# Retention and bilinear FFN on one core: q and k loads that exchange heads, GpSimd on 128 partitions, large buffers at multiples of 512 bytes

## The chip, the cores and the metric

One core of one Trainium2 chip. The metric is the device time of the kernel in microseconds. The engines are TensorE (PE, its weight loads PEld), VectorE (DVE), ScalarE (ACT), GpSimd (POOL) and SyncE (SP), which only issues DMAs here.

## The reference

```
B, H, S, D = 8, 8, 576, 64
scores = q @ k^T / sqrt(D)
gamma  = 1 - 2 ** (-5 - arange(H))
ret    = scores * where(i >= j, gamma ** (i - j), 0)      # i: query, j: key
x      = (ret @ v) with heads side by side -> [B*S, 512]   # 4608 tokens
out    = ((x @ w_a) * (x @ w_b)) @ w_out                   # 512 -> 1536 -> 512
```

Inputs and output are float32, and the kernel multiplies in bf16.

## The kernel before

The retention is computed in its recurrent form: inside a stretch of 64 tokens by scores, across stretches by a state of 64 x 64 per head. Tokens go in pairs of 128-token tiles (256 tokens). Pairs 0 to 5 belong to the first three batches; 15 and 17 (`LEFT`) collect the last 64 tokens of four batches each. The FFN runs in blocks of 512 tokens. It is PE's main work; three later blocks form sums of weights and rows on DVE, so that PE needs fewer products (`layer_mixed`, `rows_mixed`).

The program's order on every engine is written out by hand. `todo` is a list of places, counted in matmuls of 512 columns, at which `ahead`, `turn`, `stretch`, `load_pair` and `store_held` are called while the FFN's matmuls are issued. For a pair `n`:

- `load_pair(n)` issues the loads of q, k and v on SP (L171). `rows_of` gives two tiles of 128 tokens, or four of 64 for 15 and 17. A tile of `[128, 1024]` float32 holds two such tiles, each with its 8 heads of 64. The staging pool has two buffers per tensor.
- `ahead(n)` prepares operands on POOL: from pair 6 (`MIXED`) on it multiplies q by the decay table `qs2` (`decayed_queries`, L579 and L584), casts k (L605 and L609), and multiplies v by `vs2` (L616). Tokens of the second 64 partitions have the two heads of each couple exchanged in `qkb` (index `1 - r` written from `r`). So POOL works on partitions 0 to 63 and 64 to 127 in separate instructions.
- `turn(n)` transposes `qkb` by two DMAs on SP (L633) into `qkT`, and from pair 11 on then calls `load_pair(n + 2)`.
- `stretch(n, n - 1)` issues PE's products of the pair: `keyed` (L664), `matched` (scores, L735), `open_outputs` (L763) and `close_outputs` (L776).

SP takes its DMAs strictly in order, so pair 13's loads stand before pair 12's transposes. The DMAs of SP use eight semaphores in turn: each one first waits until the eighth before it has landed.

The opening (steps `STEPS`, loads L182) handles the first pairs with dummy matmuls (`warm`) between, until about 18 us. Weights come by POOL's own queue (`load_w`, `load_wo`). `pair_tables` makes `qs2` and `vs2` on ACT from `idxv`, one step at a time in the first FFN block.

`const` is the first pool in each partition's memory, and all large pools follow it. The tiles of `const` add up so that the first large buffer starts at byte 21824 of a partition, 320 past a multiple of 512; the large buffers all keep that offset.

Of the kernel before, what the change touches and what calls it, by code (L numbers as in the profile page):

```python
# [10 lines left out]
FP32 = mybir.dt.float32  # L11
BF16 = mybir.dt.bfloat16
INT32 = mybir.dt.int32
AF = mybir.ActivationFunctionType
# [4 lines left out]
def kernel(  # L19
# [10 lines left out]
    nc = tc.nc  # L30

    B, H, S, D = q.shape
    DM = H * D
# [4 lines left out]
    HP = H // 2  # L38
    scale = 1.0 / math.sqrt(D)
    gammas = [1.0 - 2.0 ** (-5.0 - h) for h in range(H)]  # L40
# [5 lines left out]
    LEFT = {NP - 3: 0, NP - 1: 1}  # L46
# [5 lines left out]
    PAIRS = [(0, 0), (1, 0), (2, 0), (0, 1), (1, 1), (2, 1)]  # L52
# [6 lines left out]
    def part_of(n):  # L59
        return PAIRS[n][1]  # L60
# [4 lines left out]
    def rows_of(n):  # L65

        if n not in LEFT:
            b, m = PAIRS[n]
            return [(kp, 0, 128, b, 256 * m + 128 * kp) for kp in (0, 1)]
        return [(i // 2, 64 * (i % 2), 64, 4 * LEFT[n] + i, S - 64)  # L70
                for i in range(4)]

    def pool(name, bufs, space=None):
        kw = {} if space is None else {"space": space}
        return ctx.enter_context(tc.tile_pool(name=name, bufs=bufs, **kw))

    const = pool("const", 1)
# [67 lines left out]
    def half(i):  # L145
        return slice(64 * i, 64 * i + 64)
# [10 lines left out]
    def staged(n, name, its_name):  # L157

        extra = n < MIXED + 3 and n % 3 == 2
        return (begin if extra else stage).tile(  # L160
            [128, 2 * DM], FP32, tag=name, name=its_name)

    def load_pair(n, which=(0, 1, 2)):
        if n >= NP:
            return
        paired.setdefault(n, {})
        for i in which:
            name, src = (("qf", q), ("kf", k), ("vf", v))[i]
            t = staged(n, name, name + "2")
            for kp, r0, m, b, s0 in rows_of(n):  # L170
                nc.sync.dma_start(  # L171
                    t[r0:r0 + m, kp * DM:(kp + 1) * DM]
                    .rearrange("p (h d) -> p h d", h=H),
                    src[b, :, s0:s0 + m, :].rearrange("h s d -> s h d"))
            paired[n][i] = t

    def load_step(n, hh, which, on=nc.sync):
# [11 lines left out]
    Q, K, V = 0, 1, 2  # L189
# [36 lines left out]
    idxp_f = const.tile([128, 2], FP32)  # L226
    nc.vector.tensor_copy(idxp_f, idxp_i)
    lgp = const.tile([128, HP], FP32)
    for c in range(HP):
        nc.vector.memset(lgp[0:64, c:c + 1], math.log(gammas[2 * c]))  # L230
        nc.vector.memset(lgp[64:128, c:c + 1], math.log(gammas[2 * c + 1]))
    biasq = const.tile([128, 1], FP32)
    nc.vector.memset(biasq, math.log(scale))
    vs = const.tile([128, H, 2], FP32)
    for h in range(H):
        nc.scalar.activation(vs[:, h, :], idxp_f, AF.Exp,
                             bias=0.0, scale=-math.log(gammas[h]))
# [10 lines left out]
    idxv = const.tile([128, 3, 2], FP32)  # L248
    vs2 = const.tile([128, 3, 2, H], FP32)

    qs2 = const.tile([128, 3, 2, H], FP32)
# [14 lines left out]

    def pair_tables(step):
        if step == 0:
            nc.vector.tensor_copy(idxv, idxv_i)
            nc.vector.tensor_scalar_add(idxv[:, 2, 1:2], idxv[:, 2, 1:2],  # L270
                                        -128.0)
            nc.vector.tensor_scalar_add(idxv[64:128, 2], idxv[64:128, 2],
                                        -64.0)
        else:
            for h in (2 * step - 2, 2 * step - 1):
                nc.scalar.activation(vs2[:, :, :, h], idxv, AF.Exp,
                                     bias=0.0, scale=-math.log(gammas[h]))
                nc.scalar.activation(qs2[:, :, :, h], idxv, AF.Exp,
                                     bias=biasq[:, 0:1],
                                     scale=math.log(gammas[h]))  # L280

    state_after = begin.tile([128, 2, HP, 128], BF16)
    own_sums = [begin.tile([128, HP, 64], FP32, name=f"own{n}")
# [280 lines left out]
    def ahead(n):  # L564


        qkb = nat.tile([128, 2, 2 * DM], BF16, tag="qkb", name="qkb2")
        vb = nat.tile([128, 2 * DM], BF16, tag="vb", name="vb2")
        halves = [slice(0, DM), slice(DM, 2 * DM)]
        whole = [slice(0, 2 * DM)]  # L570
        part = 2 if n in LEFT else part_of(n)

        def per_head(t):
            return t.rearrange("p (h d) -> p h d", d=D)

        def decayed_queries(t):
            by = qs2[:, part].rearrange("p k h -> p (k h)")
            for hs in (slice(0, H), slice(H, 2 * H)):
                nc.gpsimd.tensor_tensor(  # L579
                    per_head(qkb[0:64, Q])[:, hs], per_head(t[0:64])[:, hs],  # L580
                    by[0:64, hs].unsqueeze(2).to_broadcast([64, H, D]),
                    op=ALU.mult)
            for r in (0, 1):
                nc.gpsimd.tensor_tensor(  # L584
                    per_head(qkb[64:128, Q])[:, 1 - r::2],
                    per_head(t[64:128])[:, r::2],
                    by[64:128, r::2].unsqueeze(2).to_broadcast([64, H, D]),
                    op=ALU.mult)

        if n >= MIXED:  # L590
            decayed_queries(paired[n].pop(Q))
        if n >= BY_ACT:
            t = paired[n].pop(K)
            to, fro = (x.rearrange("p (j r d) -> p j r d", r=2, d=D)
                       for x in (qkb[64:128, K], t[64:128]))
            key_casts[n] = [
                lambda: nc.scalar.copy(qkb[0:64, K], t[0:64])] + [
                lambda r=r: nc.scalar.copy(to[:, :, 1 - r], fro[:, :, r])
                for r in (0, 1)]
            copies_due.extend([lambda: key_casts[n].pop(0)() if key_casts[n]  # L600
                               else None] * 3)
        for w in () if n >= BY_ACT else (K,) if n >= MIXED else (Q, K):
            t = paired[n].pop(w)
            for e in halves:
                nc.gpsimd.tensor_copy(qkb[0:64, w, e], t[0:64, e])  # L605
                to, fro = (x.rearrange("p (j r d) -> p j r d", r=2, d=D)
                           for x in (qkb[64:128, w, e], t[64:128, e]))
                for r in (0, 1):
                    nc.gpsimd.tensor_copy(to[:, :, 1 - r], fro[:, :, r])  # L609
        t = paired[n].pop(V)  # L610
        decay = (vs2[:, part].unsqueeze(3)
                 .to_broadcast([128, 2, H, D])
                 .rearrange("p k h d -> p (k h) d"))
        for e in halves:
            at = slice(e.start // D, e.stop // D)
            nc.gpsimd.tensor_tensor(  # L616
                vb[:, e].rearrange("p (h d) -> p h d", d=D),
                t[:, e].rearrange("p (h d) -> p h d", d=D),
                decay[:, at], op=ALU.mult)
        natural[FIRST + n, "pair"] = (qkb, vb)  # L620
# [4 lines left out]
    def turn(n):  # L625
        while key_casts.get(n):
            key_casts[n].pop(0)()
        qkb = of(natural, n)[0]
        qkT = qkt_pool.tile([128, 2, 2, HP, 128], BF16, tag="qkT",
                            name="qkT2")  # L630
        transposed[FIRST + n, "pair"] = qkT
        for w in (Q, K):
            nc.sync.dma_start_transpose(  # L633
                qkT[:, w].rearrange("p k c s -> p (k c) s"), qkb[:, w])
        if n > 10:
            load_pair(n + 2)
# [824 lines left out]


    gate = const.tile([1, 64], BF16)
    fence = const.tile([128, 2], FP32)

    def warm(count, n):

# [82 lines left out]
    for i, which in ((4, Q), (4, K), (4, V), (5, Q), (5, K), (5, V)):  # L1550
        load_step(*STEPS[i], which)
    load_pair(FIRST)
    load_pair(FIRST + 1, (Q,))


# [56 lines left out]
    todo += [(150 + 15 * step, weight_sums, (step,)) for step in range(15)]  # L1612
    todo += [(136, total_of, (2,))]
    todo += [(28 + 6 * step, pair_tables, (step,)) for step in range(5)]
    todo += [(145 + 6 * step, decays_next, (step,)) for step in range(5)]
    todo += [(170, stretch, (3, None)), (201, stretch, (4, 3)),
# [33 lines left out]
    for fn, places in ((ahead, casts), (turn, turns)):  # L1650
        todo += [(at, fn, (n,)) for n, at in places.items()]
# [46 lines left out]
```

## Time and profile before

| | us |
|---|---|
| median of 3 runs | 314.54 (314.4 to 314.97) |
| the profiled execution | 314.71 |
| its span | 313.0 |
| PE busy | 303.0 |
| DVE busy | 224.0 |
| POOL busy | 202.8 |
| ACT busy | 156.0 |
| granted clock of PE, share | 0.998 |

The span is what the profile covers of the execution, from the first to the last instruction. The page divides it in 40 slices, where each digit is the busy share in tenths. The tables by line give busy time, the mean of one instruction in ns, and the idle time of the engine just before it with what ended it. Matmuls overlap their neighbours, so one matmul's own time is longer than the distance to the next.

Where the pairs lie in this trace: POOL prepares pair 12 from 153.82 us and pair 17 from 230.83 us. PE's scores (L735) of pairs 11 to 17 begin at 162.50, 174.16, 194.29, 206.07, 226.18, 237.65 and 259.48 us.

### The profile page before, as it was taken

How to read it: one execution, taken by the hardware profiler on the slowest of the kernel's cores; microseconds unless marked ns; L12 is line 12 of the kernel's file. 1: busy time of each engine (PE TensorE's matmuls, PEld its weight loads, DVE VectorE, ACT ScalarE, POOL GpSimd, SP SyncE). 2: the span in 40 equal slices, each digit the busy share in tenths (PEclk: the TensorE clock that was granted, in tenths of full speed). 3: DMA queues.
4: the chain of work that ended last, by engine and by line, in shares of the span. 5: the costliest groups of instructions: out<-in, count | busy, mean ns of one | idle time of the engine just before them, and what ended most of it. 6: DMA issues, size and time to landing. Idle time of an engine off the chain costs nothing.

```text
span 313.0 us, 9645 instructions
## 1 busy us (share of the span) xinstructions
PE 303.0 (97%) x3922; PEld 198.6 (63%) x3955; DVE 224.0 (72%) x450; ACT 156.0 (50%) x351; POOL 202.8 (65%) x290
## 2 busy tenths in 40 slices
PE   7899999999999999999999999999999999999994
PEld 3554457868544554557874787468746875687774
DVE  5745337758757765768878886888679968877873
ACT  7755346626433554455455545544635554335530
POOL 3990079665996649867799769985999350035413
PEclk9999999999999999999999999999999999999999
DMA  8999999999999999999999989948703020013004
GB/s 213 256 202 207 247 240 198 197 216 182 208 171 231 174 204 191 218 244 285 190 260 228 179 180 227 192 83 182 213 10 70 24 112 2 2 53 85 1 2 134
DMA packets 144797, 50.97 MB, mean 163 GB/s; under 512 B 126576, under 2 KB 141680, under 8 KB 144752
## 3 DMA queue, kind: packets, MB, share of 16 engines
q1 hardware_dynamic: 138272, 45.10, 70.9%
q0 software_dynamic: 5808, 4.72, 9.6%
q8 instruction: 31, 0.51, 0.7%
q10 hardware_dynamic: 672, 0.52, 0.5%
q14 instruction: 14, 0.11, 0.1%
HBM read 37.75 MB, written 9.44 MB: 151 GB/s over the span
## 4 chain that ended last, share of the span: by engine, by line
PE 91%; DVE 2%; DMA 2%; SPq 2%; issue 2%; ACT 1%; DVEq 0%; ACTq 0%
PE m L1047 16%; PE pb L1419 13%; PE pa L1398 12%; PE pb L1284 9%; PE pa L1284 9%; PE po L1445 8%; PE lm L1227 7%; PE ls L1227 3%; DMA qf<-in_q_dram 2%; SPq L182 2%; PE la L1227 2%; PE po L933 2%; PE sc L735 2%; PE o L763 1%; PE kv L664 1%
## 5 line engine op out<-in xcount | busy, mean ns | idle before, releaser
L1424 DVE TENSOR_TENSOR hT<-ha,pb 128x512 bf16<-128x512 bf16 (+1 forms) x60 | 34.6, 579 | 32.4 <-PE pb L1419 28.4
L1419 PE MATMUL pb<-xT,wb_sb 128*128 128x512 bf16 (+1 forms) x237 | 49.9, 336 | 0.3
L1398 PE MATMUL pa<-xT,wa_sb 128*128 128x512 bf16 (+1 forms) x238 | 47.6, 326 | 0.5 <-issue 0.3
L1412 ACT CAST ha<-pa 128x512 bf16<-128x512 f32 (+1 forms) x60 | 29.8, 500 | 34.3 <-PE pa L1398 31.8
L1071 POOL TENSOR_TENSOR osb<-crossed,straight 128x256 f32<-128x256 f32 x24 | 17.5, 756 | 44.3 <-ACT crossed L1059 44.3
L1419 PEld LDWEIGHTS <-wb_sb 128*128 128x128 bf16 x240 | 23.4, 98 | 17.8 <-issue 0.5
L1398 PEld LDWEIGHTS <-wa_sb 128*128 128x128 bf16 x244 | 23.3, 98 | 16.5 <-DVE sums L691 0.2
L579 POOL TENSOR_TENSOR qkb<-qf,qs 64x512 bf16<-64x512 f32 x24 | 24.7, 1044 | 13.1 <-DMA qf<-in_q_dram 8.2
L1284 PE MATMUL pb<-xT,wb_sb 128*128 128x512 bf16 x125 | 32.1, 379 | 0.2
L616 POOL TENSOR_TENSOR vb<-vf,vs 128x512 bf16<-128x512 f32 x30 | 30.8, 1046 | 2.0 <-DMA vf<-in_v_dram 0.8
L1284 PE MATMUL pa<-xT,wa_sb 128*128 128x512 bf16 x119 | 31.4, 379 | 0.7 <-issue 0.3
L1047 PEld LDWEIGHTS <-hT 128*128 128x128 bf16 x288 | 28.1, 98 | 5.0 <-DVE hT L981 0.5
L1294 ACT CAST ha<-pa 128x512 bf16<-128x512 f32 x32 | 18.7, 585 | 24.6 <-PE pa L1284 24.6
L1297 DVE TENSOR_TENSOR hT<-ha,pb 128x512 bf16<-128x512 bf16 x32 | 21.9, 684 | 10.0 <-PE pb L1284 8.1
L609 POOL CAST qkb<-kf 64x256 bf16<-64x256 f32 x60 | 27.7, 488 | 1.5
L1445 PE MATMUL po<-wo_sb,hT 128*128 128x512 bf16 x113 | 26.7, 379 | 0.8 <-issue 0.6
L584 POOL TENSOR_TENSOR qkb<-qf,qs 64x512 bf16<-64x512 f32 x24 | 26.7, 1134 | 0.7
L1047 PE MATMUL m<-wo_sums,hsum 128*128 128x256 bf16 x216 | 25.7, 273 | 0.0
L981 DVE TENSOR_TENSOR hsum<-hT 128x512 bf16<-128x512 bf16 (+2 forms) x51 | 23.5, 493 | 0.5
L605 POOL CAST qkb<-kf 64x512 bf16<-64x512 f32 x30 | 20.3, 677 | 5.4 <-DMA kf<-in_k_dram 4.0
L1047 PEld LDWEIGHTS <-hsum 128*128 128x128 bf16 x216 | 21.1, 98 | 2.4
L1284 PEld LDWEIGHTS <-wb_sb 128*128 128x128 bf16 x128 | 12.3, 98 | 14.3
(159 smaller groups left out, 578.4 us busy)
## 6 DMA issues: line engine op xcount, KB each, us to landing
qf<-in_q_dram SPq DMA_DIRECT2D x32, 256.0 KB, 5.4
vf<-in_v_dram SPq DMA_DIRECT2D x32, 256.0 KB, 5.0
kf<-in_k_dram SPq DMA_DIRECT2D x31, 256.0 KB, 5.1
out_dram<-osb SPq DMA_DIRECT2D x9, 512.0 KB, 4.2
out_dram<-osb SPq DMA_DIRECT2D x22, 128.0 KB, 2.8
wo_sb<-in_moe_w_out_dram POOLq DMA_DIRECT2D x3, 512.0 KB, 15.9
out_dram<-osb SPq DMA_DIRECT2D x6, 256.0 KB, 4.1
qf<-in_q_dram SPq DMA_DIRECT2D x8, 128.0 KB, 3.3
```

The lines of the kernel that those rows point to most:

```text
L579: nc.gpsimd.tensor_tensor(per_head(qkb[0:64, Q])[:, hs], per_head(t[0:64])[:, hs], by[0:64, hs].unsqueeze(2).to_broadcast([64, H, D]), op= ...
L584: nc.gpsimd.tensor_tensor(per_head(qkb[64:128, Q])[:, 1 - r::2], per_head(t[64:128])[:, r::2], by[64:128, r::2].unsqueeze(2).to_broadcast( ...
L609: nc.gpsimd.tensor_copy(to[:, :, 1 - r], fro[:, :, r])
L616: nc.gpsimd.tensor_tensor(vb[:, e].rearrange("p (h d) -> p h d", d=D), t[:, e].rearrange("p (h d) -> p h d", d=D), decay[:, at], op=ALU.mult)
L1047: nc.tensor.matmul(to, rows, cols, start=(begins and p == 0), stop=True, skip_group_check=True)
L1227: nc.tensor.matmul(to[:, m], w[:, c], x[:, c], start=(way in (1, 2, 5) and m == c == 0), stop=True, skip_group_check=True)
L1284: nc.tensor.matmul(p1, w[:, c, F * 128:F * 128 + 128], xT[:, c], start=(c == 0), stop=(c == NC - 1))
L1398: nc.tensor.matmul(pa[:, at:at + width], wa_sb[:, c, fs], xT[:, c, at:at + width], start=(c == at == 0), stop=(c == NC - 1), skip_group_ch ...
L1412: nc.scalar.copy(ha[:, 0:n], pa[:, 0:n])
L1419: nc.tensor.matmul(pb[:, 0:n], wb_sb[:, c, fs], xT[:, c], start=(c == 0), stop=(c == NC - 1))
L1424: nc.vector.tensor_tensor(hT[:, F, 0:n], has[F][:, 0:n], pb[:, 0:n], op=ALU.mult)
L1445: nc.tensor.matmul(po, hT[:, F, u * 128:(u + 1) * 128], wo_sb[:, F], start=(F == 0), stop=(F == NF - 1))
```

## The change

From pair 12 (`PLACED`) on, the loads of q and k bring the heads to their exchanged places: `places_of` splits each tile of 128 tokens in three DMAs, one for the first 64 partitions with all heads, and two for the other 64 with four heads each. POOL then multiplies q and casts k on all 128 partitions at once. As the table is now read at the place where a head lies after the exchange, `qs2` gets its rates per partition, from `lgp` for even heads and from a new `lgq`, made by eight memsets on DVE, for odd ones; the older loop for pairs 6 to 11 reads the table at `1 - r`. The tile `fence` becomes part of a tile `room` of 48 columns. With `lgq` (a step of 32 bytes) and `room` the large buffers start at byte 22016, a multiple of 512.

```
+    PLACED = 12
+    def places_of(n, t, src):
+        heads = t.rearrange("p (k j r d) -> p k j r d", k=2, r=2, d=D)
+        if n in LEFT:
+            b0 = 4 * LEFT[n]
+            lower, upper = (src[b0 + a:b0 + 4:2, :, S - 64:S, :].rearrange(
+                "k (j r) s d -> s k j r d", r=2) for a in (0, 1))
+        else:
+            b, m = PAIRS[n]
+            lower, upper = (src[b, :, 256 * m:256 * m + 256, :].rearrange(
+                "(j r) (k a s) d -> a s k j r d", a=2, k=2, r=2)[a]
+                for a in (0, 1))
+        k = (0, 1)
+        return [(to[:, ks], fro[:, ks]) for ks in k for to, fro in (
+            (heads[0:64].rearrange("p k j r d -> p k (j r) d"),
+             lower.rearrange("s k j r d -> s k (j r) d")),
+            (heads[64:128, :, :, 1], upper[:, :, :, 0]),
+            (heads[64:128, :, :, 0], upper[:, :, :, 1]))]
...
     def load_pair(n, which=(0, 1, 2)):
...
+            if i == V or n < PLACED:
+                for kp, r0, m, b, s0 in rows_of(n):
...
+            else:
+                for to, fro in places_of(n, t, src):
+                    nc.sync.dma_start(to, fro)
...
+    lgq = const.tile([128, HP], FP32)
...
     def pair_tables(step):
         if step == 0:
+            for c in range(HP):
+                for i in (0, 1):
+                    nc.vector.memset(lgq[half(i), c:c + 1],
+                                     math.log(gammas[2 * c + 1 - i]))
...
-                nc.scalar.activation(qs2[:, :, :, h], idxv, AF.Exp,
-                                     bias=biasq[:, 0:1],
-                                     scale=math.log(gammas[h]))
+                nc.scalar.activation(
+                    qs2[:, :, :, h], idxv, AF.Exp, bias=biasq[:, 0:1],
+                    scale=(lgq if h % 2 else lgp)[:, h // 2:h // 2 + 1])
...
         def decayed_queries(t):
             by = qs2[:, part].rearrange("p k h -> p (k h)")
+            own = slice(0, 128 if n >= PLACED else 64)
             for hs in (slice(0, H), slice(H, 2 * H)):
                 nc.gpsimd.tensor_tensor(
-                    per_head(qkb[0:64, Q])[:, hs], per_head(t[0:64])[:, hs],
-                    by[0:64, hs].unsqueeze(2).to_broadcast([64, H, D]),
+                    per_head(qkb[own, Q])[:, hs], per_head(t[own])[:, hs],
+                    by[own, hs].unsqueeze(2).to_broadcast([own.stop, H, D]),
                     op=ALU.mult)
-            for r in (0, 1):
+            for r in () if n >= PLACED else (0, 1):
                 nc.gpsimd.tensor_tensor(
                     per_head(qkb[64:128, Q])[:, 1 - r::2],
                     per_head(t[64:128])[:, r::2],
-                    by[64:128, r::2].unsqueeze(2).to_broadcast([64, H, D]),
+                    by[64:128, 1 - r::2].unsqueeze(2).to_broadcast([64, H, D]),
                     op=ALU.mult)
...
             for e in halves:
+                if n >= PLACED:
+                    nc.gpsimd.tensor_copy(qkb[:, w, e], t[:, e])
+                    continue
...
-    fence = const.tile([128, 2], FP32)
+    room = const.tile([128, 48], FP32)
+    fence = room[:, 0:2]
```

More of the change, by code (lines that the diff above doesn't have):

```diff
@@ L169, in load_pair @@
             t = staged(n, name, name + "2")
[L170 to L174, printed above, removed]
+            if i == V or n < PLACED:
+                for kp, r0, m, b, s0 in rows_of(n):
+                    nc.sync.dma_start(
+                        t[r0:r0 + m, kp * DM:(kp + 1) * DM]
+                        .rearrange("p (h d) -> p h d", h=H),
+                        src[b, :, s0:s0 + m, :].rearrange("h s d -> s h d"))
+            else:
+                for to, fro in places_of(n, t, src):
+                    nc.sync.dma_start(to, fro)
             paired[n][i] = t
```

## The prediction

> **What bounds the kernel now.** First the page, for the engines' shares and the slices:
>
> ```profile
> span 313.0 us, 9645 instructions
> PE 303.0 (97%) x3922; PEld 198.6 (63%) x3955; DVE 224.0 (72%) x450; ACT 156.0 (50%) x351; POOL 202.8 (65%) x290
> ...
> PE   7899999999999999999999999999999999999994
> ...
> POOL 3990079665996649867799769985999350035413
> ...
> DMA  8999999999999999999999989948703020013004
> ```
>
> PE fills the span: 303.04 of 313.00 us. GpSimd (POOL) and the DMA engines are also full in long stretches. So I asked for the busy time of the engines by stretch (columns: length, then PE, PEld, DVE, ACT, POOL):
>
> ```profile
> 18.00:40.00 22.00, 21.89 (x103) 10.10 (x104) 8.56 (x15) 9.97 (x29) 6.11 (x13) 1.00 1.25 223
> 40.00:150.00 110.00, 108.42 (x1621) 66.67 (x1635) 76.48 (x147) 55.48 (x124) 82.17 (x120) 1.00 1.13 211
> 150.00:250.00 100.00, 99.31 (x1361) 70.57 (x1369) 81.22 (x150) 51.93 (x106) 83.50 (x106) 1.00 0.75 155
> 250.00:309.00 59.00, 58.55 (x582) 42.75 (x584) 44.73 (x109) 26.00 (x54) 18.30 (x26) 1.00 0.13 43
> ```
>
> The six pairs that the change touches are prepared between 142 and 241 us. There PE lacks 0.69 us in 100. Next, what PE waited for between 18 and 300 us, in whole:
>
> ```profile
> PE po L1445 <- issue: 0.6, 4, 0.2
> PE pa L1398 <- issue: 0.3, 2, 0.2
> PE pa L1284 <- issue: 0.3, 2, 0.2
> ```
>
> No wait of PE there ends with POOL, with SP or with a DMA. A faster POOL has nothing to shorten on PE. What remains outside PE is 1.5 us at the start, about 1.7 us until 18 us, 2.8 us in crumbs after that, and 3.9 us from PE's last matmul (309.1) to the end.
>
> **POOL's part.** The costs come from the page:
>
> ```profile
> L579 POOL TENSOR_TENSOR qkb<-qf,qs 64x512 bf16<-64x512 f32 x24 | 24.7, 1044 | 13.1 <-DMA qf<-in_q_dram 8.2
> L616 POOL TENSOR_TENSOR vb<-vf,vs 128x512 bf16<-128x512 f32 x30 | 30.8, 1046 | 2.0 <-DMA vf<-in_v_dram 0.8
> L609 POOL CAST qkb<-kf 64x256 bf16<-64x256 f32 x60 | 27.7, 488 | 1.5
> L584 POOL TENSOR_TENSOR qkb<-qf,qs 64x512 bf16<-64x512 f32 x24 | 26.7, 1134 | 0.7
> L605 POOL CAST qkb<-kf 64x512 bf16<-64x512 f32 x30 | 20.3, 677 | 5.4 <-DMA kf<-in_k_dram 4.0
> ```
>
> 64 partitions cost what 128 do: L579 (64x512) 1044 ns, L616 (128x512) 1046. For q, 2 x 1.044 + 2 x 1.134 = 4.36 us become 2 x 1.05 = 2.1. For k, 2 x 0.677 + 4 x 0.488 = 3.31 become 2 x 0.61 (the 128x512 cast of L371) = 1.2. That is 4.3 us a pair and 26 us for six. Its worth on the path is 0: POOL's results go to transposes and row products on which PE does not wait. The fewer POOL instructions also leave DVE alone, which is not on the path either.
>
> **SP's part.** Per pair, q and k need 12 loads instead of 4 (8 for pairs 15 and 17). Those two pairs show what a 64-partition load costs, in SP's timeline (start, length, count):
>
> ```profile
> 154.45 1.25 SPq L171 DMA_DIRECT2D qf<-in_q_dram  x2
> 155.75 1.99 SPq L171 DMA_DIRECT2D kf<-in_k_dram  x2
> 157.83 2.44 SPq L171 DMA_DIRECT2D vf<-in_v_dram  x2
> 160.38 1.56 SPq L997 DMA_DIRECT2D out_dram<-osb  x2
> 162.04 5.45 SPq L633 DMA_TRANSPOSE qkT<-qkb  x2
> ...
> 178.61 2.78 SPq L171 DMA_DIRECT2D qf<-in_q_dram  x4
> ```
>
> Twelve of them run from 178.61 to 186.84, 0.68 us each. The tightest user is pair 12: its scores (L735) begin at 174.16, and in the trace its second transpose lands at 169.5. Queued ahead of it on SP from 142.80 are the loads of pairs 12 and 13, pair 11's transposes and two stores, and nobody else issues them. If issuing sets the pace: 28 x 0.68 + 4 x 1.25 (transposes; their shortest is 1.232) + 2 x 0.52 (stores at 186.95) = 25.1 us, so 167.9, and 2 us to land: 169.9. If all the old waiting stays and 16 issues come on top: 169.5 + 16 x 0.68 = 180.4. I take 170 to 173, near the low end: the old 12 loads took 13.2 us, 1.1 each, where 0.57 is the least, so half of it was waiting for bytes that the smaller loads move while SP issues. So PE finds pair 12 ready, with 1 to 4 us left, and the cost taken is 0. Pair 13's use is at 194.3, 14's at 206.1 against 196.6 landed, 16's at 237.7 against 227.7; these have 9 us or more. Loads that arrive later meet a POOL that has 4.3 us more room per pair.
>
> **DVE's and ACT's part.** Eight memsets of `lgq` stand before `idxv` on DVE at 24.29 us. Their like (L230, L231) start 0.10 us apart, so 0.8 us. Behind them wait two products of hT (24.87) and the table activations on ACT, with an `ha` copy (26.20) behind those. The first bank that they free is needed at 27.9 by PE: the products would end at 26.95 instead of 26.15, the `ha` copy at 27.6, needed at 28.75. Cover is about 0.9 us; cost 0. The activations keep shape and count.
>
> **The addresses.** In the built program the large buffers start at 320 past a multiple of 512 bytes in each partition, afterwards at 0. The offset among them stays. No row shows another alignment, so the price is bounded. The trace's packets take 18 ns for 256 bytes, 27 for 512, 44 for 1024, 84 for 2048, 159 for 4096, and 9 for the 4-byte semaphore writes. That fits two readings equally: 9 ns per packet plus 9 per 256 bytes, or 9 ns per 256-byte block touched, of which an unaligned packet touches one more. By the first the change gives 0, by the second 9 ns a packet. Only the opening can use it, where the loads are the pace (12 loads land 0.9 us apart). There two waits on the path end with a DMA:
>
> ```profile
> 12.13 0.62 ACT L371 CAST qkb<-qf 128x512 bf16<-128x512 f32 x1 [0.23 <-DMA qf<-in_q_dram]
> ...
> 7.49 0.40 PE L389 MATMUL tp<-identity,qkb 128*128 128x128 bf16 x4 [0.20 <-POOL qkb L371]
> ```
>
> The first ends directly with a load, the second with POOL's cast of one. All other waits until 18 us end with ACT or DVE, whose chains would run on as they are. So any speed of loads is worth 0 to 0.43 us. I take 0.2, the middle, since the rows support both readings. If engines paid for the alignment too, PE would show it: matmuls of 512 and 256 columns start 216.1 and 109.2 ns apart, 2.7 ns over the columns at both lengths, and transposes, whose moving operand lies elsewhere, also at 56 for 53.3. I see no price there.
>
> The Trainium skill ("DMA: Bandwidth & Descriptors", How a descriptor splits into AXI transactions) counts 32-byte beats and lets an unaligned start pay for the bytes below it. By my estimate from that, 18 beats become 16 in the opening's packets, and the opening would gain the full 0.43 us; no run here shows it yet.
>
> **Sum.** Profiled execution 314.71 us (span 313.0, 1.7 around it): 0 (POOL) + 0 (SP) + 0 (DVE) - 0.2 = 314.5. The median of the runs, 314.54, lies 0.17 below that execution, so 314.3.
>
> **Rivals.**
> 1. *The addresses pay on the whole path.* Opening 0.43, the tail's stores 0.1, and some 0.3 of the crumbs between 60 and 80 us, where PE stands 0.31 us at 61 while DMA is full: -0.8, so 313.7. For: DMA is full until 190 us, and PE's crumbs lie mostly there. Against: PE's named waits are "issue".
> 2. *SP delays pair 12 (slower).* More loads than SP can issue push the transposes of pair 12 past 174.16. It decides from (172.1 - 142.8 - 6.1) / 28 = 0.83 us per load. At 0.90 the transposes land 2 us late, PE waits 2 us once: 316.5; at 0.86, 0.8 us late, 315.3. The worst end above, 180.4, is 6.2 us late. For: between 144.48 and 148.15 two loads took 3.57 us, and pair 17's twelve ran at 0.72. Against: 0.68 at pair 15. The Trainium skill ("SBUF — State Buffer", Can I just issue two DMAs to hit both halves?) advises against this very split: two transfers to the halves run one after the other. Here the halves' cost is already in the 0.68.
> 3. *The change does little that can be seen:* the forecast with the first reading of the packets, 314.5.
>
> **How the numbers follow.** What a measurement can tell from no change is about 0.2%, 0.63 us. The forecast and rival 3, within 0.2%: 0.43. Rival 1, mostly beyond 0.63: 0.33, since the price of the addresses is the least known term. Rival 2 and small losses like it: 0.24. The range reaches down to rival 1 with a margin of 0.3, 313.4, and up to a stall of 0.9 us, 315.4; the longer stalls and a larger gain are the 2 in 10 left out. The likeliest case alone is 313.9 to 314.7.
>
> **What would show it.** POOL's busy time about 177 us, with 128x512 at L579's and L605's successors near 1.05 and 0.61 us. SP's loads at 0.68 us each from pair 12 on. No wait of PE before L735's twelfth group; if one stands near 174 us, rival 2 is right. Packets of 256 bytes still at 18 ns mean the first reading, about 9 to 16 the second. First matmuls of L1419 earlier than 18.2 us by 0.2 to 0.4. I am wrong if matmuls start at another pace than 216.1 ns, or PE's last matmul moves by over 0.6 us without one of these waits.

## The result, and the profile after

| | median, us | profiled execution, us | its span |
|---|---|---|---|
| before | 314.92 (22 runs, 314.4 to 316.2) | 314.71 | 313.0 |
| changed | 315.98 (22 runs, 315.07 to 318.55) | 316.34 | 314.6 |

The ratio is 1.0034, 95% interval 1.0021 to 1.0047: the changed kernel is 1.07 us slower. The forecast was 314.3 with a range up to 315.4.

In the changed kernel all lines lie lower in the file: the loads L171 became L193 (old form) and L199 (new form), the transposes L633 became L667, scores L735 are L769, L776 is L810, the products of q L579 are L610, the casts of k L605 are L637 (128 partitions) and L639. First its page:

```profile
span 314.6 us, 9677 instructions
...
PE 304.6 (97%) x3922; PEld 200.1 (64%) x3955; DVE 222.0 (71%) x458; ACT 155.9 (50%) x351; POOL 175.9 (56%) x254
...
POOL 4990088595996589953794069505960350035413
...
DMA  7999999998969999996969685959596020012004
```

POOL lost 26.9 us of work, and the DMA engines' row has 8s and 6s where it had 9s. Its two new groups of POOL, from the list by line and shape:

```profile
L610 POOL TENSOR_TENSOR qkb<-qf,qs 128x512 bf16<-128x512 f32 x12 | 12.2, 1037 | 0.0
L637 POOL CAST qkb<-kf 128x512 bf16<-128x512 f32 x12 | 7.0, 606 | 0.0
```

So all that was meant to be saved was saved. The busy time by stretch (columns as before the change) shows that PE had nothing of it:

```profile
40.00:150.00 110.00, 108.42 (x1619) 66.81 (x1633) 76.74 (x146) 55.14 (x124) 82.46 (x119) 1.00 0.98 207
150.00:250.00 100.00, 99.17 (x1352) 70.19 (x1359) 77.51 (x148) 51.91 (x106) 54.48 (x70) 1.00 0.75 156
```

POOL falls from 83.50 to 54.48 us between 150 and 250 us, PE goes from 99.31 to 99.17. The DMA engines carry as much as before between 40 and 150 us in less time: share 1.13 before, 0.98 now. PE's last matmul moved from 309.08 to 310.44 us. Laying the starts of PE's instructions in the two traces side by side shows where: the changed kernel is 0.23 us behind at the end of the opening and only 0.06 at 141 us. The other 1.30 us come in the runs of 64x64 matmuls (scores, state products, outputs of two pairs) at 142, 162, 174, 206, 226 and 238 us. The run at 206 us, PE's timeline of the changed kernel (start, length, matmuls in the group):

```profile
206.71 0.61 PE L769 MATMUL sc<-qkT 64*64 64x64 bf16 x32
207.12 0.67 PE L810 MATMUL o<-sT,vb 64*64 64x64 bf16 x32
```

The same two groups before:

```profile
206.07 0.49 PE L735 MATMUL sc<-qkT 64*64 64x64 bf16 x32
206.37 0.47 PE L776 MATMUL o<-sT,vb 64*64 64x64 bf16 x32
```

They are 0.12 and 0.20 us longer, and no wait stands ahead of either. In the records of single PE instructions, weight loads included, nearly all of the excess is two holes: starts 91 and 189 ns apart, at 206.75 and 207.32 us, where the others are at most 21 ns apart. What SP does meanwhile:

```profile
205.84 0.61 SPq L199 DMA_DIRECT2D qf<-in_q_dram  x1
206.50 2.98 SPq L199 DMA_DIRECT2D kf<-in_k_dram  x3
```

Before, SP issues nothing there. From 142 to 237 us its DMA instructions now take 88 us, where they took 68. And at 238.7 us there is one wait of 0.3 us on a DMA. The view of L769 has it:

```profile
its engine sat idle before it (us, times) until:
  DMA qkT<-qkb: 0.3, 1
```

The chain that ended last, asked for 225 to 245 us (start, length, what), passes through it:

```profile
231.93 1.56 SPq L667
...
233.58 5.40 DMA qkT<-qkb
...
239.03 0.45 PE sc L769 x32
```

Pair 16's transposes, issued at 221.76 and 224.67 us before, now leave SP behind the 16 loads of pair 17 (218.43 to 229.90 us), land at 238.98, and PE wanted them 0.3 us earlier. SP's timeline of the changed kernel there (x4 are the transposes of pairs 16 and 17):

```profile
218.43 3.96 SPq L199 DMA_DIRECT2D qf<-in_q_dram  x6
...
231.14 7.88 SPq L667 DMA_TRANSPOSE qkT<-qkb  x4
```

### The profile page after: what moved, and what is told of

It reads as the page before. It is cut to its first block, busy times and chain, and to the rows that moved or that the text cites. A ratio compares the mean times of both kernels' runs of the same rounds, so it can differ in the third digit from the quotient of the medians.

```text
span 314.6 us, 9677 instructions
## 1 busy us (share of the span) xinstructions
PE 304.6 (97%) x3922; PEld 200.1 (64%) x3955; DVE 222.0 (71%) x458; ACT 155.9 (50%) x351; POOL 175.9 (56%) x254
## 4 chain that ended last, share of the span: by engine, by line
PE 85%; DVE 4%; SPq 3%; DMA 3%; issue 2%; POOL 2%; ACT 1%; DVEq 0%; ACTq 0%
PE m L1081 15%; PE pb L1453 13%; PE pa L1432 12%; PE po L1479 8%; PE pb L1318 7%; PE pa L1318 7%; PE lm L1261 5%; PE ls L1261 3%; SPq L199 2%; DMA qkT<-qkb 2%; PE po L967 2%; PE sc L769 2%; PE w L1505 2%; PE o L810 1%; PE la L1261 1%
## 5 line engine op out<-in xcount | busy, mean ns | idle before, releaser
L1432 PEld LDWEIGHTS <-wa_sb 128*128 128x128 bf16 x244 | 23.3, 98 | 16.6 <-DVE sums L725 0.2
L650 POOL TENSOR_TENSOR vb<-vf,vs 128x512 bf16<-128x512 f32 x30 | 31.8, 1079 | 1.5 <-DMA vf<-in_v_dram 0.8
L610 POOL TENSOR_TENSOR qkb<-qf,qs 64x512 bf16<-64x512 f32 (+1 forms) x24 | 24.7, 1046 | 10.9 <-DMA qf<-in_q_dram 3.9
L1015 DVE TENSOR_TENSOR hsum<-hT 128x512 bf16<-128x512 bf16 (+2 forms) x51 | 20.7, 438 | 0.5
L1318 PEld LDWEIGHTS <-wa_sb 128*128 128x128 bf16 x128 | 12.1, 98 | 12.4
L778 DVE TENSOR_TENSOR sT<-sc,mask 128x512 bf16<-128x512 f32 x30 | 19.9, 684 | 0.0
L725 DVE TENSOR_TENSOR sums<-kv,sums 128x256 f32<-128x256 f32 x44 | 18.6, 423 | 1.6
```

The lines of the kernel that those rows point to most:

```text
L610: nc.gpsimd.tensor_tensor(per_head(qkb[own, Q])[:, hs], per_head(t[own])[:, hs], by[own, hs].unsqueeze(2).to_broadcast([own.stop, H, D]), ...
L650: nc.gpsimd.tensor_tensor(vb[:, e].rearrange("p (h d) -> p h d", d=D), t[:, e].rearrange("p (h d) -> p h d", d=D), decay[:, at], op=ALU.mult)
L1015: lambda e=ways[i]: nc.vector.tensor_tensor(*e[:3], op=e[3]))
L1318: nc.tensor.matmul(p1, w[:, c, F * 128:F * 128 + 128], xT[:, c], start=(c == 0), stop=(c == NC - 1))
L1432: nc.tensor.matmul(pa[:, at:at + width], wa_sb[:, c, fs], xT[:, c, at:at + width], start=(c == at == 0), stop=(c == NC - 1), skip_group_ch ...
```

## The experiments

Runs 1 to 4, 5 to 8 and 9 to 11 shared a chip, each group with runs of the kernel before beside it, and the ratios are to those.

| run | edit | median, us | ratio, 95% |
|---|---|---|---|
| 1 | before, new addresses | 314.48 | 0.9985, 0.9974 to 0.9995 |
| 2 | changed, old addresses | 318.17 | 1.0117, 1.0089 to 1.0145 |
| 3 | changed, old POOL work | 315.02 | 1.0012, 0.9999 to 1.0025 |
| 4 | changed, old loads | 315.01 | 1.0003, 0.9990 to 1.0015 |
| 5 | run 1, loads cut by halves | 314.68 | 0.9985, 0.9968 to 1.0002 |
| 6 | run 1, loads cut by heads | 314.21 | 0.9980, 0.9970 to 0.9990 |
| 7 | changed, pair 17 behind | 315.57 | 1.0016, 1.0001 to 1.0031 |
| 8 | before, addresses at 256 | 314.64 | 0.9985, 0.9977 to 0.9994 |
| 9 | run 4, quarters of heads | 314.81 | 0.9988, 0.9967 to 1.0009 |
| 10 | run 4, pair 17 behind | 314.79 | 0.9989, 0.9966 to 1.0013 |
| 11 | before, addresses at 128 | 314.78 | 0.9987, 0.9967 to 1.0007 |
| 12 | run 9 as [4,64] | 321.43 | 1.0186, 1.0152 to 1.0219 |

**Runs 1 to 4: which part loses.** Each part of the change alone, or undone.

Run 1:

```
-    fence = const.tile([128, 2], FP32)
+    room = const.tile([128, 56], FP32)
+    fence = room[:, 0:2]
```

> The kernel before, with a room of 56 columns ahead of the large buffers, so that they start at a multiple of 512 bytes as in the changed kernel; loads and POOL stay old. Three theories of the 1.07 us that the change lost. Loads: the 64-partition loads cost it, by holes of 53 to 189 ns in PE's runs of 64x64 matmuls while SP issues them and by pair 16's transposes coming late (335 ns of waiting); then this kernel is at before or up to 0.4 us under it, 314.5 to 314.9 us, with packets of 512 bytes at 27 ns in the opening. Addresses: the new addresses cost it; then 316.0. POOL: work on 128 partitions costs it; then 314.9 as before.

Run 2:

```
-    room = const.tile([128, 48], FP32)
+    room = const.tile([128, 128], FP32)
```

> The changed kernel, with a room of 128 columns, so that the large buffers start at 320 past a multiple of 512 bytes as in the kernel before; loads and POOL stay changed. Loads: 316.0 to 316.5 us, the holes and the late pair 16 stay or grow, since packets are slower under load again (512 bytes near 32 ns in the opening). Addresses: back to 314.9. POOL: 316.0.

Run 3:

```
-            own = slice(0, 128 if n >= PLACED else 64)
+            for own in (half(0), half(1)) if n >= PLACED else (half(0),):
...
-                    nc.gpsimd.tensor_copy(qkb[:, w, e], t[:, e])
+  (one cast of [64,512] for the lower half, two of [64,256] for the upper)
```

> The changed kernel with its 64-partition loads and its addresses, but POOL works on q and k of pairs 12 to 17 in instructions of 64 partitions, as many and as long as before. Loads: 316.0 us or a little more (POOL is done up to 4.3 us later per pair, which can delay a transpose), with the holes in PE's 64x64 runs at the same places. Addresses: 316.0. POOL: 314.9.

Run 4:

```
-            if i == V or n < PLACED:
+            if True:
```

> The changed kernel with its addresses and POOL on 128 partitions, but q and k of pairs 12 to 17 are loaded by the old 128-partition loads; it leaves out the exchange of heads in these pairs. Loads: 314.5 to 314.9 us, none of the new holes, pair 16's transposes in time. Addresses: 316.0. POOL: 316.0.

The theory that the new addresses cost falls with run 1: they gain 0.15%, 0.47 us. The loads theory gets its sign, and no more: it gave run 2 at most 316.5, and it is 318.17; it gave run 3 316.0, and it is 315.02; it gave run 4 at most 314.9, and it is 315.01. Run 2 has in full what was the slower rival of the prediction, at its place. The waits of PE between 18 and 300 us, and SP's timeline:

```profile
PE sc L769 <- DMA qkT<-qkb: 2.0, 2, 1.7
```

```profile
142.98 4.62 SPq L199 DMA_DIRECT2D qf<-in_q_dram  x6
...
168.65 5.30 SPq L667 DMA_TRANSPOSE qkT<-qkb  x2
```

Pair 12's second transpose ends its issue at 173.95 and lands at 176.2 us; PE's starts are 1.84 us apart at 174.40. In the changed kernel the same loads begin at 141.30 and these transposes are issued from 166.12 to 170.80, as SP's timeline has it:

```profile
141.30 4.59 SPq L199 DMA_DIRECT2D qf<-in_q_dram  x6
...
166.12 4.68 SPq L667 DMA_TRANSPOSE qkT<-qkb  x2
```

So the addresses are worth 0.47 us without the new loads and some 2.6 us (1.0117 against 1.0034) with them: they make good most of what the loads would have cost. In run 3 the holes are all there (1.25 us in eleven of them from 140 us on, against 0.85 in nine in the changed kernel), but pair 16's transposes land at 236.4 and 237.3 us and PE does not wait. Run 4 shows three holes at 206 us (95, 69, 81 ns) that run 1 lacks, below loads of [8,64] of pair 17, which are as old as the kernel: POOL was ready earlier, SP came to them at 202.39 us and not at 209.47, and so they met the run. A fourth hole (83 ns at 174.47 us) lies behind a load of [8,64] of pair 15.

**Where a hole lies.** In all 46 holes (two starts in a run of 64x64 matmuls that are 37 ns or more apart) that follow a load or store (no semaphore in between, from 50 us on, all 14 profiles of this case, the half-speed run at 181 us of run 12 left out), I took the time from the start of SP's last issue to the end of the hole. 37 lie between 325 and 350 ns, while the starts of these holes vary from 139 to 310 ns. Chance would spread these ends over the 0.6 us of an issue. So the issue on SP stops PE's dispatch until 0.34 us after its start, if PE dispatches something just then. Beside longer matmuls nothing of it is seen: those of 512 columns start 216 ns apart in the median with and without such an issue, those of 256 columns 109 ns apart.

**Runs 5 and 6: halves or mere number.** On top of run 1, for pairs 12, 13, 14 and 16:

```
+                for at in (0, 1):
+                    ps, hs = half(at), slice(0, 8)                    # run 5
+                    ps, hs = slice(0, 128), slice(4 * at, 4 * at + 4) # run 6
+                    nc.sync.dma_start(to[ps, hs], fro[ps, hs])
```

> The kernel before at the new addresses (314.48 us), with each load of q and k of pairs 12, 13, 14 and 16 cut in two by partitions, 64 and 64, and no heads exchanged: 8 loads of [8,64] in place of 4 of [8,128]; POOL stays old. So far 17 of 31 loads on 64 partitions, and 1 of 20 on 128, whose issue fell into a run of 64x64 matmuls left a hole of 39 to 241 ns in it. Halves theory (a load on 64 partitions makes the holes): 0.4 to 0.8 us over it, 314.9 to 315.3, with holes near 142, 162, 174 and 206 us. Count theory (any load issued in a run does, and there were only more of them): the same here. Backlog theory (only SP's delay matters, holes are chance): 314.5.

> As the run by halves, but each of these loads is cut in two by heads: 8 loads of [4,128], all on 128 partitions, as many issues and as many bytes. Halves theory: 314.4 to 314.7 us, at most one hole of under 100 ns after 140 us. Count theory: 314.9 to 315.3 with holes as by halves. Backlog theory: 314.5 in both.

Both stay within their intervals of run 1, so neither time decides. Run 5's forecast of 314.9 or more missed. POOL kept its old pace, and only four of the new issues fell into a run of 64x64 matmuls, and one left a hole (76 ns). In run 6 one of four did (110 ns, forecast under 100). That needed a kernel in which SP is busy all along, run 9.

**Runs 7 and 10: the queue.** `turn(15)` issues pair 17's loads behind pair 15's transposes; here `turn(16)` does, on top of the changed kernel (7) and of run 4 (10):

```
-        if n > 10:
+        if n > 10 and n != 15:
             load_pair(n + 2)
+        if n == 16:
+            load_pair(17)
```

> The changed kernel with the loads of pair 17 (16 issues) put behind pair 16's transposes on SP instead of ahead of them. Backlog theory for the wait of 335 ns at 238.7 us: pair 16's transposes are issued at about 226 us instead of 231 to 236, land before 237.7, and the wait is gone: 0.3 to 0.5 us under the changed kernel, 315.5 to 315.7, with the holes at 142 to 207 us still there. If POOL or something else makes these transposes late, the wait stays and the time is 316.0.

> The run with POOL alone (315.01 us; old loads, exchange left out), with pair 17's 12 loads of [8,64] behind pair 16's transposes. In that run POOL was done earlier, so pair 17's loads were issued from about 202 us on instead of 209.5 and met the run of 64x64 matmuls at 205.5 us: holes of 95, 69 and 81 ns. Theory that POOL's speed costs only by what it lets SP issue into a run: these three go, 314.5 to 314.8 us. Theory that POOL's wide instructions themselves cost: 315.0 as before.

In run 7 pair 16's transposes are issued from 220.38 to 223.04 us, the wait at 238.7 is gone, and the median is 0.41 us under the changed kernel, as the backlog theory had it; holes at 142, 174, 207 and 227 us are still there, though fewer: five of 0.63 us together, for nine of 0.85. In run 10 the three holes at 206 go, and pair 17's loads meet the run at 225.5 us instead and leave one of 127 ns. The time, 314.79, can't be told from run 4's 315.01.

**Runs 9 and 12: the same loads in two shapes.** Run 4 with eight loads for each q and k of pairs 12, 13, 14 and 16, of the same bytes each:

```
+                    for h0 in (0, 2, 4, 6):                          # run 9
+                        nc.sync.dma_start(to[:, h0:h0 + 2], fro[:, h0:h0 + 2])
+                    for ps in (half(0), half(1)):                    # run 12
+                        for hs in (slice(0, 4), slice(4, 8)):
+                            nc.sync.dma_start(to[ps, hs], fro[ps, hs])
```

> The changed kernel (new addresses, POOL on 128 partitions), but q and k of pairs 12, 13, 14 and 16 are loaded by 8 loads each of [2,128] (a quarter of the heads, all partitions) in place of 6 on 64 partitions; it leaves out the exchange of heads in pairs 12 to 17, and pairs 15 and 17 keep their old loads of [8,64]. SP is then about as long at issuing per pair as in the changed kernel (16 x 0.5 us for 12 x 0.65), so issues fall into the runs of 64x64 matmuls at 142, 162 and 174 us again. In all runs so far a hole ends 0.34 us after the start of an issue on SP. Halves theory (loads on 64 partitions do it): few holes at these three runs, 314.6 to 315.2 us. Count theory (any issue does it): holes of 50 to 190 ns at these three as in the changed kernel, 315.5 to 316.

> The run by quarters of the heads (314.81 us, no hole behind any of its issues of [2,128]), with the same 8 loads for each q and k of pairs 12, 13, 14 and 16, of the same bytes each, but as [4,64]: half of the partitions and half of the heads. The exchange of heads is left out in pairs 12 to 17 here too. Halves theory: in the runs of 64x64 matmuls at 142, 162, 174 and 206 us, about half of the issues that fall into them leave a hole that ends 0.34 us after the issue's start, 0.4 us or more together, 315.2 us or more. SP then issues 16 x 0.65 = 10.4 us per pair, so a late transpose of pair 14 or 16 can add up to 1 us. Theory that the exchanged addresses in DRAM, and not the half partitions, make the holes: none, as by quarters.

Run 9, PE's timeline at the run that was at 206 us, and SP's:

```profile
205.44 0.49 PE L773 MATMUL sc<-qkT 64*64 64x64 bf16 x32
205.74 0.47 PE L814 MATMUL o<-sT,vb 64*64 64x64 bf16 x32
```

```profile
204.26 2.01 SPq L200 DMA_DIRECT2D kf<-in_k_dram  x4
```

SP issues through the whole run, and PE's groups are as long as before the change. Run 12, the same run of matmuls, 8 us later:

```profile
213.98 0.60 PE L774 MATMUL sc<-qkT 64*64 64x64 bf16 x32
```

```profile
212.57 2.59 SPq L201 DMA_DIRECT2D qf<-in_q_dram  x4
```

The hole of 86 ns is back, and each of the five runs of 64x64 matmuls at 142, 162, 202, 213 and 234 us has one (those at 202 and 234 behind the old [8,64] loads of v). No heads are exchanged in either kernel, so it is not the exchange. An issue of [2,128] took SP 0.47 us, one of [4,64] 0.62, and the queue that follows from that is the larger price; PE's waits in run 12:

```profile
PE sc L774 <- DMA qkT<-qkb: 6.5, 1, 6.5
```

This wait was not foreseen: the forecast had up to 1 us for pair 14 or 16, and it is pair 12, at 174 us. So run 12's time says nothing of the holes; its trace does.

All 14 profiles together, over the loads whose stretch of 0.08 to 0.48 us after the start lies in a run of 64x64 matmuls for 0.3 us or more:

| load on | issues in a run | with a hole | mean ns lost per issue |
|---|---|---|---|
| 64 partitions | 53 | 29 | 63 |
| 128 partitions | 61 | 5 | 6 |

The address may matter too. Four of the five holes on 128 partitions are in kernels whose large buffers don't start at a multiple of 256 bytes (before and run 11): such kernels, run 2 included, have 4 holes in 13 of these issues, the others 1 in 48. No run tells the two apart, and of run 9's shape [2,128] there are only six issues in the table. Why the partitions matter to PE's dispatch stays open. The fetch of PE's own code is not in flight at a hole: it comes in 31 packets of 16384 bytes, and those near the holes of the changed kernel start at 144.5, 177.3, 196.8, 208.0 and 227.8 us, after them. (The Trainium skill, "Runtime: NRT & Kernel Launch", Instruction fetch mechanics, names the same blocks of 16 KiB; the trace agrees.)

**Runs 8 and 11: which alignment.** Run 1 with `room` of 120 and of 88 columns, so that the buffers start at 256 and at 128 past a multiple of 512.

> The kernel before with the large buffers at 256 past a multiple of 512 bytes (before: 320; the changed kernel: 0). If a packet pays for 256-byte blocks or smaller ones, the opening's packets of 512 bytes take 27 ns as at 0, and the time is that of the first of these runs, 314.5 us. If it is multiples of 512 that count, the mean stays near 32 ns and the time is 314.8.

> The kernel before with the large buffers at 128 past a multiple of 512 bytes (320 in before, 256 and 0 in two runs of 314.5 to 314.6 us). If it is whole blocks of 256 bytes, packets of 512 bytes in the opening have a mean near 32 ns again and the time is 314.8. If blocks of 128 bytes or less count, the mean is 27 ns and the time 314.5.

SP's packets of 512 bytes until 15 us had a mean of 31.9 ns at 320 (before), 32.8 at 128, 27.1 at 256 and 27.1 at 0. Of the four offsets, the two multiples of 256 are the fast ones. Run 8's time answers to run 1's; run 11's interval holds both answers, so its verdict rests on the packets alone.

**The sum by the ratios of the table**, as shares of 314.9 us: addresses -0.47 (run 1), the new loads +0.85 (run 3 less run 1), POOL on 128 partitions with them, pair 17's loads behind, +0.13 (run 7 less run 3, within the noise), pair 17's loads ahead of pair 16's transposes +0.57 (the changed kernel less run 7): together +1.07. In another order, POOL on 128 partitions with the old loads is +0.57 (run 4 less run 1) and the new loads +0.98 (the changed kernel less run 4). Each difference has an interval of 0.5 to 0.6 us either way, so the split is rough. The traces, one of each kernel, show what the parts are made of: from 141 us on, the changed kernel falls 1.30 us behind the kernel before (nine holes, 0.85 us, and the wait, 0.34), run 3 1.32 (eleven holes, 1.25) and run 7 0.56 (five holes, 0.63).

## Why the prediction was wrong

*Right.* PE is the bound, and a faster POOL shortened nothing on it (it was not free either: run 4 less run 1 is +0.57 us, just beyond its interval). POOL's saving was 26 us by the sum, 26.9 measured; the shapes cost 1037 and 606 ns for 1050 and 610. A new load took SP 0.66 us with its gap for 0.68. Pair 12's transposes are issued by 170.80, and PE did not wait for them. DVE's memsets, at 24 us, moved nothing: the lead of before is 0.23 us at 16 us and still 0.23 at 40.

*The failed step: "13's use is at 194.3, 14's at 206.1 against 196.6 landed, 16's at 237.7 against 227.7; these have 9 us or more".* That is the slack of the old queue. 8 more issues per pair are 5 us each time, and SP, once it has no idle time left, carries them on to the next pair: pair 14's transposes landed at 204.5 in place of 196.6, pair 16's at 238.98 in place of 227.7. I summed the queue to its first user and should have summed it to the last. The wait that came of it is 0.34 us, the smaller part of what the term "0 (SP)" left out.

*The missing term, and the larger part: what an issue costs an engine that does not wait for it.* The cost of SP's part was taken as zero as long as PE finds its data. The runs show 63 ns of PE per issue on 64 partitions in a run of short matmuls. The changed kernel has nine such holes, 0.85 us. The trace of before had one, 45 ns at 194.36 us and behind a load of [8,128], too small to be read as a price; its loads of [8,64] were issued outside these runs, at 178 and 209 us.

*Rival 2* had the right mechanism and the wrong place: in the changed kernel it is pair 16, for 0.3 us. At the old addresses (run 2) it is pair 12, as written, and its point of 0.83 us per load was too high: run 2's 28 loads took 20.4 us, 0.73 each, and it was late, because the four transposes took 8.5 us and not 5.0, and its loads began 1.7 us later than those of the changed kernel. The Trainium skill's warning ("SBUF — State Buffer", Can I just issue two DMAs to hit both halves?) was set aside with the words that the halves' cost is in the 0.68. Run 12 against run 9 shows that it is not all there.

*The addresses* were mis-sized: -0.2 forecast, -0.47 measured. The bounds came from two waits that end with a load; the opening can gain more, 0.7 us (below). Of the two readings of the packets neither was right: the floor stays at 27 and 18 ns, as the first says, but at 320 many packets of 512 bytes took up to 38. The Trainium skill ("DMA: Bandwidth & Descriptors", How a descriptor splits into AXI transactions) lets a read start only at a multiple of 256 bytes and counts the bytes below an unaligned start. My estimate from that was 18 beats for 16 and the full 0.43 us, though here it is the written side that is unaligned. Run 8 and run 11 agree with the boundary. The size fits roughly: by the same estimate 20 beats at 128 past, so 1.25 and 1.13 times the aligned time; measured 1.21 (32.8 against 27.1 ns) and 1.18 (31.9). Rival 1 thus had the right sign for this part alone: run 1 is 0.15% faster.

*The sign to look for in the opening* was useless: the first matmul of L1419 came at 18.47 us, later than 18.23. The last section says why. Of the listed signs, one was met to the letter: PE's last matmul moved by over 0.6 us without one of the named waits.

## What to carry to other kernels

Sum a queue to its last user: once it has no idle time left, each added issue is handed on, and slack read from the old trace is gone. Cutting a load by partitions is dearer than cutting it by bytes within all 128: 0.62 against 0.47 us of issuing for the same bytes, and holes in runs of short matmuls on PE (29 of 53 issues). When POOL gets faster, ask what SP will then issue earlier, and into which run. Start buffers that small packets load at a multiple of 256 bytes: the padding alone (run 1) beat both kernels at 0.9985, and with loads cut by heads (run 6) the ratio is 0.9980 (0.9970 to 0.9990).

## What the runs showed of the hardware

- **An issue of a DMA on SP can stop PE's dispatch** until 0.34 us after its start, for 40 to 200 ns. In a run of 64x64 matmuls 29 of 53 loads on 64 partitions did, and 5 of 61 on 128.
- **The start of full clock varies.** The trace's record of the granted clock begins full speed between 4.5 and 7.5 us in these profiles. With aligned buffers the first matmul of L1419 (or its like) follows it: 4.55 us and 17.51 (run 8), 5.83 and 17.93 (run 1), 6.81 and 18.20 (run 3), 7.46 and 18.47 (changed), 0.33 us per us. The other aligned kernels lie near the same line. The kernel before has 4.51 and 18.23, so at the same clock the addresses gain 0.7 us in the opening, and the profile of the changed kernel hid that by a late clock. The Trainium skill ("TensorE: Matmul & The Clock Gate", Part 1) says that the window is free-running and varies from run to run; the traces agree.
- **A long wait costs twice.** Behind run 12's wait of 6.5 us, PE came back at half clock. Its busy time by stretch, with the granted clock as third figure from the end:

```profile
174.00:181.00 7.00, 0.53 (x54) 0.41 (x43) 3.16 (x5) 0.16 (x1) 2.90 (x2) 0.71 1.06 272
181.00:182.00 1.00, 0.82 (x64) 0.82 (x54) 0.00 (x0) 0.12 (x1) 0.00 (x0) 0.50 0.46 102
```

The record has half clock from 176.97 to 183.79 us. Against the kernel before, PE was 6.60 us behind at the end of that wait, and 7.89 us behind when full clock was back.
